# Attention with a following mixture of adapters: loads, stores and mixture steps moved to fixed places, x transposed by DMA

## The chip, the cores and the metric

One core of a Trainium2 chip. The metric is the device time of one execution in microseconds (us); lower is better. The span in a profile is about 2 us shorter than the time of the same run (286.4 against 288.2 us before), because it counts from the first to the last instruction.

Engines are named as in the profile: PE is TensorE (PEld its weight loads), DVE is VectorE, ACT is ScalarE, POOL is GpSimd. SPq is the queue of SyncE, from which nearly all DMAs are issued (36.2 of the 38.2 MB that the kernel before moves), one after another in program order.

A run over 1.5% above the fastest of its kernel is called slow here and is left out of the ratios.

## The reference, cut to what matters

```python
# B, H, S, D = 8, 8, 576, 64
scores = q @ k.T / sqrt(D) + bias_table[bucket(i - j)]   # per batch and head
x = softmax(scores) @ v                                  # [B*S, H*D] = [4608, 512]
logits = x @ w_gate                                      # 8 adapters, the 2 best are kept
out = x + sum over the 2 kept e of  w_e * (x @ A[e]) @ B[e]
```

## The kernel before

A pair is two heads of one batch; there are 32 pairs, four to a batch. Pair i goes through five groups g = 0..4 (scores of 128 keys, exp on ACT, multiplication by exp(bias) on DVE, called a band). While pair i makes its scores, TensorE also multiplies the probabilities of pair i-1 with v (`pv`), and at the end of the slot DVE normalises them into x (`norm`). A batch of x is complete after four pairs; then its twelve mixture steps are put into a list and taken from it one by one, in groups 1, 2 and 3 of the next pairs.

```python
    def load_v(b, h0, h1):                 # 16 DMAs of 64 KB
        vr = v[b, h0:h1, :S4, :].rearrange("h (t p j) d -> j t p h d", t=4, j=4)
        for j in range(4):
            for t in range(4):
                nc.sync.dma_start(out=vfs[b][j * 32:(j + 1) * 32, t, h0:h1, :],
                                  in_=vr[j, t])
    # ... cut ...
    def norm(i):
        # ... cut ...
        nc.vector.reciprocal(rc, at(acc, D, (SLOT, 5), (D1, 2)))
        rm = sp.tile([128, 5, 2], FP32, name="rm", tag="rm")
        nc.vector.tensor_tensor(rm, rc, mask, op=ALU.mult)
        nc.vector.tensor_tensor(xs[b][:, :, 2 * hp:2 * hp + 2, :], ...)   # x
    # ... cut ...
    def m_x(b, half):                      # x transposed: 8 products on PE, one DVE copy
        ps = acp.tile([128, 4, 256], BF16, name="xps", tag="acc")
        for t2 in range(2):
            for c in range(4):
                nc.tensor.transpose(ps[:, c, t2 * 128:(t2 + 1) * 128],
                                    x[:, 2 * half + t2, 2 * c:2 * c + 2, :], ident)
        nc.vector.tensor_copy(xT[:, :, half * 256:(half + 1) * 256], ps)
    # ... cut ...
    def m_out(b, t):                       # one row tile: result, then four stores of 64 KB
        o = op.tile([128, Dm], FP32, name="o", tag="o")          # 3 buffers
        nc.vector.tensor_tensor(o, ps, xs[b][:, t]..., op=ALU.add)
        for j in range(4):
            nc.sync.dma_start(out=orr[j], in_=o[j * 32:(j + 1) * 32])
    # ... cut ...
    for i in range(NPAIR + 1):
        b, hp = divmod(i, HP)
        if i < NPAIR:
            if i == 1:
                load_weights()                         # adapters A, B and the gate
            if hp == 0 and b + 1 < B:
                load_kq(b + 1, 0, H)
                load_v(b + 1, 0, H)                    # sixteen in one go
                load_tails(b + 1)
            if i + 2 < NPAIR:
                cast_kq(i + 2)                         # GpSimd
            cast_v(i)                                  # GpSimd
            if i == 2:
                cast_weights()                         # GpSimd
            if hp == 1 and b + 1 < B:
                load_vtails(b + 1)                     # GpSimd; waits for pv of two pairs ago
            if i < HP - 1:
                bias_pair(i + 1, nc.gpsimd)
        for g in range(5):
            # ... qk, transposes, pv ...
            if g in (1, 2, 3) and i > 0:
                if queue:
                    queue.pop(0)()                     # the next mixture step
```

The softmax here doesn't subtract the row's maximum and nothing guards it: scores larger than these inputs give would overflow.

## Time and profile before

289.8 us (median of the first three runs, 288.9 to 290.3).

| before | value |
|---|---|
| span of the profiled run | 286.4 us |
| busy share PE / DVE / ACT / POOL | 68 / 71 / 57 / 39% |
| start of the x tile of pair 0 / 3 / 31 | 29.8 / 56.8 / 266.0 us |
| 28 pairs, from x of pair 3 to x of pair 31 | 209.2 us |
| from the start of the last x to the end | 20.4 us |

The start times of the DVE operation that writes x, once per pair, cut the run into stages. The busy lines of the page of the kernel before:

```profile
PE 195.4 (68%) x2603; PEld 132.1 (46%) x2608; DVE 204.6 (71%) x496; ACT 163.6 (57%) x184; POOL 113.1 (39%) x218
```

No engine is full over the whole run. But in stretches without holes DVE is, and PE nearly. Next is the table of stretches; each line gives the stretch, then busy us (and instructions) of PE, PEld, DVE, ACT and POOL, the granted clock of PE, a DMA share and GB/s:

```profile
110.00:115.00 5.00, 2.08 (x31) 1.44 (x29) 0.07 (x1) 2.86 (x3) 3.02 (x5) 1.00 1.37 238
115.00:120.00 5.00, 0.00 (x0) 0.00 (x0) 0.00 (x0) 0.00 (x0) 0.00 (x0) 0.62 0.80 153
120.00:125.00 5.00, 2.18 (x19) 1.36 (x18) 4.04 (x10) 0.00 (x0) 0.00 (x0) 0.50 0.52 137
...
150.00:155.00 5.00, 4.91 (x81) 3.58 (x78) 4.97 (x11) 4.20 (x5) 3.19 (x5) 1.00 1.22 185
```

At 150 us PE and DVE are both nearly always busy. At 115 us every engine stands still for 5 us, and in the next 5 us the clock is half. Why it stands still is in the timeline of DVE, and then of SPq, around that time (start, duration, engine, line, operation; in brackets the idle time before it and what ended it):

```profile
109.38 0.68 DVE L489 TENSOR_TENSOR o<-dl,x 128x512 f32<-128x512 f32 x1
120.89 0.69 DVE L506 COPY o<-dlt 128x512 f32<-128x512 f32 x1 [10.82 <-DMA out_dram<-o]
```

```profile
105.30 12.28 SPq L92 DMA_DIRECT2D vf<-in_v_dram  x16
117.68 5.57 SPq L494 DMA_DIRECT2D out_dram<-o  x12
```

DVE has nowhere to write: its three output buffers wait for stores, and the stores wait behind sixteen v loads, which take 12.3 us to issue. The waits of all engines list this three times: two long ones, of 10.8 and 10.4 us, and one of 1.4 us at the very end. They also list a similar wait of GpSimd for the adapter weights near 40 us (engine, line, releaser: us in total, times, longest):

```profile
DVE o L506 <- DMA out_dram<-o: 22.6, 3, 10.8
...
POOL Ab L265 <- DMA A_f<-in_moe_A_dram: 8.0, 1, 8.0
```

### The profile page before, as it was taken

What the parts mean: (1) busy time and instruction counts of PE and PEld (TensorE: products, weight loads), DVE (VectorE), ACT (ScalarE), POOL (GpSimd) and SP (SyncE); (2) the same over time, 40 slices, a digit from 0 to 9 for tenths busy, and PEclk for the clock granted to TensorE, in tenths of its full rate; (3) what the DMA queues carried; (4) which work ended last, traced back from release to release, by engine and by line L of the source; (5) the groups of instructions that cost most, each with busy time, mean ns of one, the idle gap of its engine ahead of it and who ended that gap; (6) DMA issues with size and microseconds to landing.
All of it is one profiled execution on the core that took longest, in us unless ns stands there. A gap on an engine that the chain in (4) does not pass through costs nothing.

```text
span 286.4 us, 6863 instructions
## 1 busy us (share of the span) xinstructions
PE 195.4 (68%) x2603; PEld 132.1 (46%) x2608; DVE 204.6 (71%) x496; ACT 163.6 (57%) x184; POOL 113.1 (39%) x218
## 2 busy tenths in 40 slices
PE   2149760997797686089698869239689778887550
PEld 1025430665565464066466556127466555655410
DVE  5217823998998973178889887067979999889750
ACT  2238860778696746048398727307859677785000
POOL 8263906947523914005704760400923380020100
PEclk9999996699999979669799968859979999999955
DMA  8969969931397649730389549950249432401424
GB/s 156 208 153 266 221 104 286 175 58 13 64 312 115 136 113 288 151 85 2 37 283 144 134 75 299 147 144 17 18 124 278 115 86 64 117 8 39 111 73 111
DMA packets 78169, 38.17 MB, mean 133 GB/s; under 512 B 55984, under 2 KB 73400, under 8 KB 78136
## 3 DMA queue, kind: packets, MB, share of 16 engines
q1 hardware_dynamic: 65080, 36.16, 51.0%
q0 software_dynamic: 13056, 1.58, 9.5%
q8 instruction: 20, 0.33, 0.5%
q14 instruction: 13, 0.11, 0.1%
HBM read 29.84 MB, written 9.45 MB: 137 GB/s over the span
## 4 chain that ended last, share of the span: by engine, by line
DVE 35%; PE 19%; DMA 15%; SPq 15%; issue 7%; ACT 3%; POOL 3%; DVEq 0%; ACTq 0%; POOLq 0%
DMA vf<-in_v_dram 9%; PE pv L358 8%; DVE x L383 7%; SPq L92 7%; DVE kqT L281 3%; DMA out_dram<-o 3%; SPq L494 3%; DVE o L489 3%; DMA g_d<-ge 2%; DVE rm L382 2%; PE sc L315 2%; PE xps L399 2%; SPq L84 2%; PE sc L319 2%; DVE rc L380 2%
## 5 line engine op out<-in xcount | busy, mean ns | idle before, releaser
L315 PE MATMUL sc<-kqT 64*128 64x512 bf16 x256 | 53.0, 412 | 1.1 <-ACT p_286 L327 0.7
L279 PE MATMUL kqps<-ident,kqn 128*128 128x128 bf16 x256 | 23.2, 237 | 24.3 <-POOL kqn L128 19.4
L279 PEld LDWEIGHTS <-kqn 128*128 128x128 bf16 x256 | 16.1, 105 | 33.5 <-POOL kqn L128 22.4
L399 PE MATMUL xps<-ident,x 128*128 128x128 bf16 x128 | 12.7, 242 | 23.9 <-DVE o L506 18.7
L281 DVE COPY kqT<-kqps 128x1024 bf16<-128x1024 bf16 x32 | 21.8, 683 | 10.0 <-PE kqps L279 10.0
L383 DVE TENSOR_TENSOR x<-pv,rm 128x640 bf16<-128x640 f32 x32 | 26.4, 825 | 1.1
L128 POOL CAST kqn<-kf 128x512 bf16<-128x512 f32 x31 | 24.1, 776 | 5.8 <-DMA kf<-in_k_dram 5.7
L128 POOL CAST kqn<-qf 128x512 bf16<-128x512 f32 x31 | 22.1, 711 | 9.2 <-DMA qf<-in_q_dram 9.2
L489 DVE TENSOR_TENSOR o<-dl,x 128x512 f32<-128x512 f32 x32 | 21.7, 685 | 3.6 <-PE dl L487 2.3
L399 PEld LDWEIGHTS <-x 128*128 128x128 bf16 x128 | 8.5, 106 | 29.0 <-issue 22.2
L487 PE MATMUL dl<-Bb,zT 128*128 128x512 bf16 x31 | 13.1, 431 | 10.4 <-DVE zT L481 6.6
L506 DVE COPY o<-dlt 128x512 f32<-128x512 f32 x4 | 2.8, 691 | 23.4 <-DMA out_dram<-o 22.6
L315 PEld LDWEIGHTS <-kqT 64*128 64x128 bf16 x256 | 12.5, 94 | 15.0 <-issue 3.2
L319 PE MATMUL sc<-kqT,tlT 128*128 128x512 bf16 x32 | 13.1, 411 | 5.2 <-ACT p_4328 L327 0.8
L300 ACT ACTIVATE ptl<-tsc 128x512 bf16<-128x512 f32 x8 | 4.8, 594 | 19.9 <-PE tsc L297 19.9
L323 PEld LDWEIGHTS <-kqT 128*128 128x128 bf16 x128 | 10.6, 104 | 10.6 <-issue 7.2
L116 POOL DMA_DIRECT2D vt_99<-in_v_dram x8 | 4.9, 621 | 22.7 <-PE pv L358 22.7
L439 ACT ACTIVATE ex<-df 128x32 f32<-128x32 f32 (+1 forms) x12 | 2.7, 222 | 19.1 <-POOL df L433 19.1
L323 PE MATMUL sc<-tlT,kqT 128*128 128x128 bf16 x128 | 13.4, 232 | 0.0
L380 DVE RECIPROCAL rc<-pv 128x10 f32<-128x10 f32 x32 | 6.9, 216 | 8.6 <-PE pv L358 8.6
L116 POOL DMA_DIRECT2D vt_96<-in_v_dram x8 | 4.9, 618 | 19.9 <-PE pv L358 19.9
L401 DVE COPY xT<-xps 128x1024 bf16<-128x1024 bf16 x16 | 10.9, 683 | 2.1 <-PE xps L399 2.1
(792 smaller groups left out, 706.5 us busy)
## 6 DMA issues: line engine op xcount, KB each, us to landing
vf<-in_v_dram SPq DMA_DIRECT2D x128, 64.0 KB, 3.3
out_dram<-o SPq DMA_DIRECT2D x128, 64.0 KB, 1.7
kf<-in_k_dram SPq DMA_DIRECT2D x7, 1024.0 KB, 6.0
qf<-in_q_dram SPq DMA_DIRECT2D x7, 1024.0 KB, 9.3
out_dram<-o SPq DMA_DIRECT2D x8, 128.0 KB, 2.4
kf<-in_k_dram SPq DMA_DIRECT2D x1, 768.0 KB, 5.1
qf<-in_q_dram SPq DMA_DIRECT2D x1, 768.0 KB, 6.8
Mr<-g_d SPq DMA_DIRECT2D x4, 144.0 KB, 4.3
```

Source lines behind the costliest of these rows:

```text
L92: nc.sync.dma_start(out=vfs[b][j * 32:(j + 1) * 32, t, h0:h1, :], in_=vr[j, t])
L128: nc.gpsimd.tensor_copy(o, s)
L279: nc.tensor.transpose(o[:, :, j, :], n[:, w, j], ident)
L281: nc.vector.tensor_copy(t, ps)
L315: nc.tensor.matmul(sc[:, h * 512:(h + 1) * 512], lhsT=t[s, 0, g * 128:(g + 1) * 128], rhs=t[s, 1, :], start=True, stop=True)
L319: nc.tensor.matmul(sc[:, 0:512], lhsT=tt[:, 0, hp, :], rhs=t[:, 1, :], start=True, stop=True)
L323: nc.tensor.matmul(sc[:, o:o + 128], lhsT=t[:, 0, j * 128:(j + 1) * 128], rhs=tt[:, 1, hp, :], start=True, stop=True, skip_group_check=True)
L358: nc.tensor.matmul(acc[:, sl * SLOT + o:sl * SLOT + o + n], lhsT=lhsT, rhs=rhs, start=start, stop=stop, skip_group_check=True)
L383: nc.vector.tensor_tensor(xs[b][:, :, 2 * hp:2 * hp + 2, :], at(acc, 0, (SLOT, 5), (D1, 2), (1, D)), rm.unsqueeze(3).to_broadcast((128, 5, ...
L399: nc.tensor.transpose(ps[:, c, t2 * 128:(t2 + 1) * 128], x[:, 2 * half + t2, 2 * c:2 * c + 2, :], ident)
L487: nc.tensor.matmul(ps, lhsT=zT[:, t, :], rhs=Bb, start=True, stop=True)
L489: nc.vector.tensor_tensor(o, ps, xs[b][:, t].rearrange("p h d -> p (h d)"), op=ALU.add)
```

## The change

Its intent: spread the DMAs so that nothing urgent stands behind a long row of others; give every mixture step a fixed slot with a distance between dependent steps; take the transposes of x off PE and DVE by a transposing DMA; and make the first v values arrive already cast. The core of the diff, with cuts marked:

```diff
-    def load_v(b, h0, h1):
+    def load_v(b, js):                       # a quarter (four DMAs) per pair
...
-        for t2 in range(2):                  # m_x: still there, for the last batch only
+    def m_xdma(b):
+        xT = xp.tile([128, 16, 128], BF16, name="xT", tag="xT")
+        st[(b, "xT")] = xT
+        nc.sync.dma_start_transpose(
+            out=xT, in_=xs[b][:, 0:4].rearrange("p t h d -> p (t h d)"))
...
-        o = op.tile([128, Dm], FP32, name="o", tag="o")
+        if t == 0:
+            st[(b, "o")] = op.tile([128, 4, Dm], FP32, name="o", tag="o")
...
+        if t % 2 == 1:                       # stores of two row tiles at once
...
         nc.vector.reciprocal(rc, at(acc, D, (SLOT, 5), (D1, 2)))
+        between()                            # a band multiply
         rm = sp.tile([128, 5, 2], FP32, name="rm", tag="rm")
...
+    # first v values: sixteen casting loads issued by GpSimd
+            nc.gpsimd.dma_start(out=vns[0][j * 32:(j + 1) * 32, t, :, :D], in_=...)
...
+        i0 = HP * (b + 1) + 1                # slots of the mixture of batch b
+        if b < B - 1:
+            at_slot(0, 0, lambda: m_xdma(b))
+        else:
+            at_slot(0, 1, lambda: m_x(b, 0))
+            at_slot(0, 2, lambda: m_x(b, 1))
+        at_slot(1, 1, lambda: m_logits(km, st[(b, "xT")], 4))
+        # gate steps at (1,3), (1,4), (2,0), (2,1), (2,2); z at (2,1), (2,2);
+        # zT at (2,4); outputs at (3,1) to (3,4)
...
             if hp == 0 and b + 1 < B:
                 load_kq(b + 1, 0, H)
-                load_v(b + 1, 0, H)
+            if b + 1 < B:
+                load_v(b + 1, (hp,))
```

The casts of k, q and v were also spread over the groups of a pair, and the loads of k and q of batch 0 were cut into four.

More of the change, by code (lines that the diff above doesn't have):

```diff
@@ L79, in alloc_loads @@
         kfs[b] = (kf, qf)
-        vfs[b] = ldp.tile([128, 4, H, D], FP32, name="vf", tag="vf")
+        if b > 0:
+            vfs[b] = ldp.tile([128, 4, H, D], FP32, name="vf", tag="vf")
     def load_kq(b, h0, h1):
@@ L86, in load_kq @@
                 in_=src[b, h0:h1, :S4, :].rearrange("h (p j) d -> p h (j d)", j=4))
-    def load_v(b, h0, h1):
-        vr = v[b, h0:h1, :S4, :].rearrange("h (t p j) d -> j t p h d", t=4, j=4)
-        for j in range(4):
+    def load_v(b, js):
+        vr = v[b, :, :S4, :].rearrange("h (t p j) d -> j t p h d", t=4, j=4)
+        for j in js:
             for t in range(4):
-                nc.sync.dma_start(out=vfs[b][j * 32:(j + 1) * 32, t, h0:h1, :],
+                nc.sync.dma_start(out=vfs[b][j * 32:(j + 1) * 32, t, :, :],
                                   in_=vr[j, t])
@@ L119, with cast_kq @@
     kqn = {}
-    def cast_kq(i, engs=None):
+    def cast_kq(i, w, eng=None):
         b, hp = divmod(i, HP)
-        t = knp.tile([128, 2, 4, 2, D], BF16, name="kqn", tag="kqn")
-        for w in range(2):
-            o = t[:, w].rearrange("p j h d -> p h j d")
-            s = kfs[b][w][:, 2 * hp:2 * hp + 2, :].rearrange("p h (j d) -> p h j d", j=4)
-            if engs is None:
-                nc.gpsimd.tensor_copy(o, s)
-            elif engs[w] == "v":
-                nc.vector.tensor_copy(o, s)
-            else:
-                for h in range(2):
-                    nc.scalar.copy(o[:, h], s[:, h])
-        kqn[i] = t
+        if w == 0:
+            kqn[i] = knp.tile([128, 2, 4, 2, D], BF16, name="kqn", tag="kqn")
+        o = kqn[i][:, w].rearrange("p j h d -> p h j d")
+        s = kfs[b][w][:, 2 * hp:2 * hp + 2, :].rearrange("p h (j d) -> p h j d", j=4)
+        if eng is nc.scalar:
+            for h in range(2):
+                nc.scalar.copy(o[:, h], s[:, h])
+        else:
+            (eng or nc.gpsimd).tensor_copy(o, s)
     def cast_v(i):
@@ L146 @@
         nc.vector.memset(t, 0.0)
+    load_kq(0, 2, 4)
+    load_kq(0, 4, 6)
     load_tails(0)
-    load_v(0, 0, H)
-    load_kq(0, 2, H)
+    nc.vector.memset(vns[0][:, :, :, D:D1], 1.0)
+    for j in range(4):
+        for t in range(4):
+            nc.gpsimd.dma_start(
+                out=vns[0][j * 32:(j + 1) * 32, t, :, :D],
+                in_=v[0, :, t * 128:(t + 1) * 128, :]
+                .rearrange("h (p j) d -> j p h d", j=4)[j])
     C = 255
@@ L155 @@
     nc.vector.memset(g_sb, 0.0)
-    cast_kq(0, "va")
+    cast_kq(0, 0, nc.vector)
+    cast_kq(0, 1, nc.scalar)
     bsub = cp.tile([H, NB], FP32, tag="bsub")
@@ L188 @@
     MHr = cp.tile([128, HP, 192], BF16, tag="MHr")
-    for h0, h1 in ((0, 2), (2, H)):
+    for h0, h1 in ((0, 2), (2, 4), (4, H)):
         for j in range(4):
@@ L200 @@
                                 ap=[[1, 64], [1024, HP], [1, 192]]))
+        if h0 == 2:
+            load_kq(0, 6, H)
     M = cp.tile([128, H, 3, 128], BF16, tag="M")
@@ L230 @@
         nc.gpsimd.memset(vt[64:128, :, 2 * D + 1:2 * D1], 1.0)
-    for vn in vns:
-        nc.gpsimd.memset(vn[:, :, :, D:D1], 1.0)
+    nc.gpsimd.memset(vns[1][:, :, :, D:D1], 1.0)
     load_vtails(0)
@@ L372, in pv, with norm @@
         mm(0, 2 * D1, lhsT, vt[:, hp, :], False, True)
-    def norm(i):
+    def norm(i, between):
         b, hp = divmod(i, HP)
@@ L393, in m_x @@
         if half == 0:
-            st[(b, "xT")] = xp.tile([128, 4, S4], BF16, name="xT", tag="xT")
-        xT = st[(b, "xT")]
-        ps = acp.tile([128, 4, 256], BF16, name="xps", tag="acc")
-        for t2 in range(2):
-            for c in range(4):
-                nc.tensor.transpose(ps[:, c, t2 * 128:(t2 + 1) * 128],
-                                    x[:, 2 * half + t2, 2 * c:2 * c + 2, :], ident)
-        nc.vector.tensor_copy(xT[:, :, half * 256:(half + 1) * 256], ps)
+            st[(b, "xT")] = xp.tile([128, 16, 128], BF16, name="xT", tag="xT")
+        ps = acp.tile([128, 8, 128], BF16, name="xps", tag="acc")
+        for n in range(8):
+            c = n % 4
+            nc.tensor.transpose(ps[:, n, :], x[:, 2 * half + n // 4, 2 * c:2 * c + 2, :],
+                                ident)
+        nc.vector.tensor_copy(st[(b, "xT")][:, half * 8:half * 8 + 8, :], ps)
     def m_xtail(b):
@@ L416, in m_xtail, with m_logits @@
         st[(b, "xT", "t")] = xT
-    def m_gate(key, xT, nt):
+    def m_logits(key, xT, nt):
         lp = acp.tile([128, nt, E], FP32, name="lp", tag="acc")
@@ L422, in m_gate @@
             for c in range(4):
-                nc.tensor.matmul(lp[:, t, :], lhsT=xT[:, c, t * 128:(t + 1) * 128],
+                nc.tensor.matmul(lp[:, t, :], lhsT=xT[:, 4 * t + c, :],
                                  rhs=Wb[:, c, :], start=first, stop=(c == 3),
@@ L431, in m_gate @@
             nc.vector.max(out=m8[:, t, :], in_=lg[:, t, :])
-        df = sp.tile([128, nt, E], FP32, name="df", tag=f"df{nt}")
-        nc.gpsimd.tensor_tensor(df, lg, m8[:, :, 0:1].to_broadcast((128, nt, E)),
-                                op=ALU.subtract)
-        mk = sp.tile([128, nt, E], FP32, name="mk", tag=f"mk{nt}")
-        nc.vector.tensor_tensor(mk, lg, m8[:, :, 1:2].to_broadcast((128, nt, E)),
-                                op=ALU.is_ge)
-        ex = sp.tile([128, nt, E], FP32, name="ex", tag=f"ex{nt}")
@@ L439, in m_gate @@
-        nc.scalar.activation(ex, df, ACT.Exp)
-        nc.gpsimd.tensor_tensor(mk, mk, ex, op=ALU.mult)
-        st[key + ("mk",)] = mk
-    def m_gate2(key, nt):
-        mk = st.pop(key + ("mk",))
-        sm = sp.tile([128, nt], FP32, name="sm", tag=f"sm{nt}")
-        nc.vector.tensor_reduce(sm, mk, axis=AX.X, op=ALU.add)
-        nc.vector.reciprocal(sm, sm)
-        gate = sp.tile([128, nt, E], BF16, name="gate", tag=f"gate{nt}")
-        nc.gpsimd.tensor_tensor(gate, mk, sm.unsqueeze(2).to_broadcast((128, nt, E)),
-                                op=ALU.mult)
-        st[key + ("gate",)] = gate
+        st[key] = dict(lg=lg, m8=m8)
@@ new lines, in m_gate @@
+    def m_gate(key, nt, part):
+        d = st[key]
+        if part == 0:
+            df = sp.tile([128, nt, E], FP32, name="df", tag=f"df{nt}")
+            nc.gpsimd.tensor_tensor(
+                df, d["lg"], d["m8"][:, :, 0:1].to_broadcast((128, nt, E)),
+                op=ALU.subtract)
+            mk = sp.tile([128, nt, E], FP32, name="mk", tag=f"mk{nt}")
+            nc.vector.tensor_tensor(
+                mk, d["lg"], d["m8"][:, :, 1:2].to_broadcast((128, nt, E)),
+                op=ALU.is_ge)
+            d.update(df=df, mk=mk)
+        elif part == 1:
+            ex = sp.tile([128, nt, E], FP32, name="ex", tag=f"ex{nt}")
+            nc.scalar.activation(ex, d["df"], ACT.Exp)
+            d["ex"] = ex
+        elif part == 2:
+            nc.gpsimd.tensor_tensor(d["mk"], d["mk"], d["ex"], op=ALU.mult)
+        elif part == 3:
+            sm = sp.tile([128, nt], FP32, name="sm", tag=f"sm{nt}")
+            nc.vector.tensor_reduce(sm, d["mk"], axis=AX.X, op=ALU.add)
+            nc.vector.reciprocal(sm, sm)
+            d["sm"] = sm
+        else:
+            gate = sp.tile([128, nt, E], BF16, name="gate", tag=f"gate{nt}")
+            nc.gpsimd.tensor_tensor(
+                gate, d["mk"], d["sm"].unsqueeze(2).to_broadcast((128, nt, E)),
+                op=ALU.mult)
+            st[key + ("gate",)] = gate
@@ L460, in m_z @@
             for c in range(4):
-                nc.tensor.matmul(zp[:, t, :], lhsT=xT[:, c, t * 128:(t + 1) * 128],
+                nc.tensor.matmul(zp[:, t, :], lhsT=xT[:, 4 * t + c, :],
                                  rhs=Ab[:, c, :], start=(t == 0 and c == 0),
@@ L487, in m_out @@
         nc.tensor.matmul(ps, lhsT=zT[:, t, :], rhs=Bb, start=True, stop=True)
-        o = op.tile([128, Dm], FP32, name="o", tag="o")
-        nc.vector.tensor_tensor(o, ps, xs[b][:, t].rearrange("p h d -> p (h d)"),
+        if t == 0:
+            st[(b, "o")] = op.tile([128, 4, Dm], FP32, name="o", tag="o")
+        o = st[(b, "o")]
+        nc.vector.tensor_tensor(o[:, t], ps, xs[b][:, t].rearrange("p h d -> p (h d)"),
                                 op=ALU.add)
-        n0 = b * S + t * 128
-        orr = out[n0:n0 + 128, :].rearrange("(u j) d -> j u d", j=4)
-        for j in range(4):
-            nc.sync.dma_start(out=orr[j], in_=o[j * 32:(j + 1) * 32])
+        if t % 2 == 1:
+            n0 = b * S + (t - 1) * 128
+            orr = out[n0:n0 + 256, :].rearrange("(t u j) d -> j u t d", t=2, j=4)
+            for j in range(4):
+                nc.sync.dma_start(out=orr[j], in_=o[j * 32:(j + 1) * 32, t - 1:t + 1])
     def m_outt(b):
@@ L504, in m_outt @@
                              start=False, stop=(e == 1), skip_group_check=True)
-        o = op.tile([128, Dm], FP32, name="o", tag="o")
+        o = op.tile([128, Dm], FP32, name="ot", tag="ot")
         nc.vector.tensor_copy(o, ps)
@@ L509, in m_outt, with mixture, at_slot, both @@
             nc.sync.dma_start(out=out[n0:n0 + 64, :], in_=o[e * 64:(e + 1) * 64])
-    def pieces(b):
+    events = {}
+    def mixture(b):
         km, kt = (b, "m"), (b, "t")
         tail = b % 2 == 1
-        def xT(t=None):
-            return st[(b, "xT", "t") if t else (b, "xT")]
-        def step(f, ft=None):
-            def run():
-                f()
-                if tail and ft:
-                    ft()
-            return run
-        return [
-            step(lambda: m_x(b, 0)),
-            step(lambda: m_x(b, 1)),
-            step(lambda: None, lambda: m_xtail(b)),
-            step(lambda: m_gate(km, xT(), 4), lambda: m_gate(kt, xT(1), 1)),
-            step(lambda: m_gate2(km, 4), lambda: m_gate2(kt, 1)),
-            step(lambda: m_z(km, xT(), 0)),
-            step(lambda: m_z(km, xT(), 1)),
-            step(lambda: m_zT(km, 4), lambda: m_z(kt, xT(1), 2)),
-            step(lambda: m_out(b, 0), lambda: m_zT(kt, 1)),
-            step(lambda: m_out(b, 1)),
-            step(lambda: m_out(b, 2)),
-            step(lambda: m_out(b, 3), lambda: m_outt(b)),
-        ]
+        i0 = HP * (b + 1) + 1
+        def at_slot(di, g, f, only_tail=False):
+            if tail or not only_tail:
+                events.setdefault(5 * (i0 + di) + g, []).append(f)
+        def both(f):
+            f(km, 4)
+            if tail:
+                f(kt, 1)
+        if b < B - 1:
+            at_slot(0, 0, lambda: m_xdma(b))
+        else:
+            at_slot(0, 1, lambda: m_x(b, 0))
+            at_slot(0, 2, lambda: m_x(b, 1))
+        at_slot(0, 4, lambda: m_xtail(b), True)
+        at_slot(1, 1, lambda: m_logits(km, st[(b, "xT")], 4))
+        at_slot(1, 1, lambda: m_logits(kt, st[(b, "xT", "t")], 1), True)
+        for n, g in enumerate((8, 9, 10, 11, 12)):
+            at_slot(0, g, lambda n=n: both(lambda k, nt: m_gate(k, nt, n)))
+        at_slot(2, 1, lambda: m_z(km, st[(b, "xT")], 0))
+        at_slot(2, 2, lambda: m_z(km, st[(b, "xT")], 1))
+        at_slot(2, 3, lambda: m_z(kt, st[(b, "xT", "t")], 2), True)
+        at_slot(2, 4, lambda: m_zT(km, 4))
+        at_slot(3, 0, lambda: m_zT(kt, 1), True)
+        at_slot(3, 1, lambda: m_out(b, 0))
+        at_slot(3, 2, lambda: m_out(b, 1))
+        at_slot(3, 3, lambda: m_out(b, 2))
+        at_slot(3, 4, lambda: m_out(b, 3))
+        at_slot(4, 4, lambda: m_outt(b), True)
@@ L541 @@
     NPAIR = B * HP
-    queue = []
+    for b in range(B):
+        mixture(b)
     late = None
@@ L545 @@
     tail_transposes(0)
-    cast_kq(1)
+    cast_kq(1, 0)
+    cast_kq(1, 1)
     for i in range(NPAIR + 1):
@@ L554 @@
                 load_kq(b + 1, 0, H)
-                load_v(b + 1, 0, H)
                 load_tails(b + 1)
-            if i + 2 < NPAIR:
-                cast_kq(i + 2)
-            cast_v(i)
+            if b + 1 < B:
+                load_v(b + 1, (hp,))
             if i == 2:
@@ L568 @@
                 qk(i, g)
-            if g == 0 and i + 1 < NPAIR:
-                transposes(i + 1)
+                if g == 0 and b > 0:
+                    cast_v(i)
+                if g in (1, 2) and i + 2 < NPAIR:
+                    cast_kq(i + 2, g - 1)
             if g == 0 and i < NPAIR and hp == 0:
                 tail_scores(b)
-            if g in (1, 2, 3) and i > 0:
-                if queue:
-                    queue.pop(0)()
-                pv(i - 1, g - 1)
+            if g == (0 if i > 3 else 3) and i + 1 < NPAIR:
+                transposes(i + 1)
+            for f in events.pop(5 * i + g, ()):
+                f()
+            for sl in ((), (0,), (1,), (2, 3), (4,))[g] if i > 0 else ():
+                pv(i - 1, sl)
             if g == 3 and hp == HP - 1 and b + 1 < B:
@@ L579 @@
             if g == 4 and i > 0:
-                pv(i - 1, 3)
-                pv(i - 1, 4)
-                norm(i - 1)
-                if i % HP == 0:
-                    queue += pieces(i // HP - 1)
-            if late:
+                norm(i - 1, late or (lambda: None))
+            elif late:
                 late()
@@ L594, in late @@
                         tail_band(i // HP)
-    for f in queue:
-        f()
+    for key in sorted(events):
+        for f in events[key]:
+            f()
 _INS = ['q', 'k', 'v', 'bias_table', 'moe_w_gate', 'moe_A', 'moe_B']
```

## The prediction

> **What bounds it now.** The span is 286.4 us; no engine is full (VectorE 71%, TensorE 68%, ScalarE 57%, GpSimd 39%). Where nothing blocks, a head pair with mixture work takes 5.7 to 5.9 us (finished x tiles in the timeline, 150.04 to 155.80) with VectorE busy 4.9 of every 5 us (stretch table): VectorE bounds the good stretches. The rest is holes:
> - 39 to 49 us: GpSimd waits 8.0 us for the adapter weights, queued behind sixteen v loads (14.5 us of issue); bias tiles and casts stand behind it.
> - 110 to 121 and 181 to 190 us: VectorE waits for an output buffer (waits: o on out_dram, 22.6 us in 3), because stores stand behind sixteen v loads.
> - After each hole the granted clock is 0.50 for some 5 us.
> - Once per batch mixture steps wait for one another on TensorE (1.3 us twice), and a band multiply takes 2.1 instead of 0.41 us, five times, under three GpSimd casts back to back. [...]
>
> **What the change does.**
> 1. v loads come four per pair, weights after the first four; `o` holds a batch. The three holes go: 28 us, plus 2 us of slow clock each: about 32 us.
> 2. Mixture steps in fixed slots, a dependent step at least one group later: 1 to 2 us a batch, about 10 us in all.
> 3. x transposed by DMA for seven batches of eight: VectorE loses 14 copies of 0.68 us (9.6 us), TensorE 112 transposes about 0.06 us apart (7 us). About 5 us on the path.
> 4. A band multiply between the reciprocal and its use: about 2 us.
> 5. Start: sixteen casting loads on GpSimd at about 0.63 us (as its other loads take) are 10 us, so pair 1's cast comes at about 21 instead of 18 us; the bias table comes earlier (its store issues at about 8 instead of 11 us). These cancel: x of pair 0 at about 29 us, as before.
> 6. End: same chain, about 20 us after the last x.
>
> **Cost.** The DMA transpose of 512 KB must be back about 6 us after x. [...] Four v loads (3.3 us to land) and stores stand just ahead. [...]
>
> **Sum.** 289.8 - 32 - 10 - 5 - 2 + 7 = about 248 us. From the other side: x of pair 3 at 46 us, 28 pairs at 6.3, 20 us of end, 3 of launch: 245. Prediction 248 us, 80% range 233 to 268. Chances: faster by over 2% 0.94, within 2% 0.03, slower 0.03.
>
> **What would show it.** No wait of VectorE for stores; no wait over 3 us for the weights; clock 1.0 from 30 us to the end of the pairs; x tiles 5.6 to 6.4 us apart; VectorE busy about 193 us; x of pair 0 at 28 to 31 us, of pair 31 at 220 to 228; [...], any stall standing on the gate logits' first product.
>
> **What would make it wrong.** [...] The sixteen casting loads take much longer, delaying pair 1. VectorE and GpSimd collide more as both get denser. The start keeps a hole for the weights.

The sum came to 248 us. Its term + 7 is the estimate of TensorE's stall behind the DMA transposes.

## The result, and the profile after

256.3 us median (255.4 to 257.9, 4 runs); before in the same rounds 289.4. The ratio is 0.886 (95% interval 0.881 to 0.892). A ratio is the mean time of one kernel's fast runs over that of the other's of the same rounds, so it is not quite the ratio of the medians. To compare kernels of different rounds I multiply each ratio by 288.4 us, about the median of before; the changed kernel is then 255.6 us.

| | before | after | predicted |
|---|---|---|---|
| time, us | 289 | 256.3 | 248 (233 to 268) |
| x of pair 0, us | 29.8 | 32.6 | 28 to 31 |
| x of pair 3, us | 56.8 | 52.7 | 46 |
| 28 pairs, us | 209.2 | 184.2 | 176 |
| end after the last x, us | 20.4 | 17.6 | 20 |
| busy DVE, us | 204.6 | 195.0 | 193 |

The busy line of the page after:

```profile
PE 187.8 (74%) x2496; PEld 123.7 (49%) x2496; DVE 195.0 (77%) x483; ACT 162.7 (64%) x184; POOL 117.3 (46%) x229
```

The wait of DVE for stores is gone from the list. Stores and four v loads now take turns (timeline of SPq):

```profile
103.63 4.10 SPq L523 DMA_DIRECT2D out_dram<-o  x6
107.77 2.33 SPq L93 DMA_DIRECT2D vf<-in_v_dram  x4
110.21 1.90 SPq L404 DMA_TRANSPOSE xT<-x  x1
```

The weights are waited for about half as long as before, and a new wait has come, of the first product that needs the transposed x (waits):

```profile
PE lp L438 <- DMA xT<-x: 11.9, 6, 3.1
...
POOL Ab L273 <- DMA A_f<-in_moe_A_dram: 4.5, 1, 4.5
```

One instance in full, batch 1. First DVE, then SPq, then PE in the timeline after:

```profile
76.90 0.82 DVE L392 TENSOR_TENSOR x<-pv,rm 128x640 bf16<-128x640 f32 x1
```

```profile
78.67 1.99 SPq L93 DMA_DIRECT2D vf<-in_v_dram  x4
80.76 2.48 SPq L404 DMA_TRANSPOSE xT<-x  x1
```

```profile
82.01 0.39 PE L323 MATMUL sc<-kqT 64*128 64x512 bf16 x2
85.46 0.56 PE L438 MATMUL lp<-Wb,xT 128*128 128x8 bf16 x16 [3.06 <-DMA xT<-x]
```

x is complete at 77.7 us. The queue first finishes its stores and issues four v loads, so the transpose is issued 3.0 us after x was ready, at 80.76. It lands 4.66 us later by the chain that ended last, at 85.42, and the logits start at 85.46. TensorE has then stood idle for 3.06 us. The stretches after it show what follows (columns as above):

```profile
82.00:86.00 4.00, 0.94 (x25) 0.64 (x24) 1.76 (x5) 1.51 (x2) 0.00 (x0) 1.00 0.91 180
86.00:90.00 4.00, 4.00 (x54) 2.90 (x51) 2.67 (x12) 2.15 (x3) 1.46 (x3) 0.65 0.41 94
90.00:94.00 4.00, 4.00 (x54) 2.50 (x53) 3.41 (x12) 3.90 (x6) 2.36 (x7) 0.93 0.98 312
```

The clock is 0.65 in the mean of the next 4 us: it falls to 0.50 at 87.2 us, 1.7 us after the logits started, and stays there for 3.4 us. PE is now full (4.00 of 4 us) at a low clock, and DVE, which should be the limit, idles a third of the time (busy 2.67 of 4 us). Here a gap of 3.06 us was followed by the low clock; this instance alone does not show that the gap brought it.

The clock records show more than this one instance. After 50 us and until the pairs end, the clock of this kernel falls seven times, each time to 0.50 for 3.4 us (the last time for 6.8), and the falls stand a multiple of 3.41 us apart. In the 3.41 us before each fall PE was busy 44 to 62%. Three of the seven have a wait for the transposed x in those 3.41 us (3.06, 1.30 and 3.09 us), four have none; x_on_pe, below, has no such wait and still falls twice. So it need not be a stop of 3 us: before the four falls without that wait PE was busy 44 to 57% of the 3.41 us. What decides whether the clock falls is not shown.

### The profile page after: what moved, and what is told of

The parts are those of the page before. It is cut to its first block, busy times and chain, and to the rows that moved or that the text cites. A ratio compares the mean times of both kernels' runs of the same rounds, so it can differ in the third digit from the quotient of the medians.

```text
span 254.5 us, 6519 instructions
## 1 busy us (share of the span) xinstructions
PE 187.8 (74%) x2496; PEld 123.7 (49%) x2496; DVE 195.0 (77%) x483; ACT 162.7 (64%) x184; POOL 117.3 (46%) x229
## 4 chain that ended last, share of the span: by engine, by line
PE 43%; DVE 32%; DMA 13%; POOL 7%; issue 2%; ACT 1%; DVEq 0%; POOLq 0%; ACTq 0%
PE pv L366 17%; DMA xT<-x 11%; PE sc L323 9%; DVE p L350 6%; DVE x L392 6%; DVE o L517 5%; PE zp L487 3%; DVE p L342 3%; DMA tl<-in_q_dram 3%; DVE rm L391 3%; PE dl L513 3%; PE kqps L287 3%; DVE kqT L289 2%; POOL vn L152 2%; DVE tlT L298 2%
## 5 line engine op out<-in xcount | busy, mean ns | idle before, releaser
L335 ACT ACTIVATE p<-sc 128x1024 bf16<-128x1024 f32 x160 | 155.8, 1024 | 65.7 <-PE sc L323 36.1
L366 PE MATMUL pv<-vn,p 128*128 128x65 bf16 (+1 forms) x1152 | 68.2, 206 | 12.6 <-DVE x L392 12.5
L366 PEld LDWEIGHTS <-p 128*128 128x128 bf16 x1280 | 59.0, 104 | 37.4 <-issue 18.9
L350 DVE TENSOR_TENSOR p<-p,M 128x512 bf16<-128x512 bf16 (+1 forms) x128 | 66.2, 533 | 3.3 <-POOL M L223 2.7
L366 PE MATMUL pv<-vt,p 128*128 128x130 bf16 x128 | 29.8, 232 | 2.4 <-DVE p L342 2.4
L453 POOL TENSOR_TENSOR df<-lg,m 128x32 f32<-128x32 f32 (+1 forms) x12 | 3.5, 293 | 60.6 <-DVE lg L443 31.8
L287 PEld LDWEIGHTS <-kqn 128*128 128x128 bf16 x256 | 15.8, 101 | 24.6 <-POOL kqn L132 11.3
L117 POOL DMA_DIRECT2D vt<-in_v_dram x16 | 9.8, 621 | 32.6 <-PE pv L366 32.6
L137 POOL CAST vn<-vf 128x512 bf16<-128x512 f32 x28 | 20.5, 733 | 0.0
L342 DVE TENSOR_TENSOR p<-p,M 128x256 bf16<-128x256 bf16 x32 | 18.5, 579 | 0.1
L327 PE MATMUL sc<-kqT,tlT 128*128 128x512 bf16 x32 | 13.7, 427 | 0.0
L438 PE MATMUL lp<-Wb,xT 128*128 128x8 bf16 x128 | 4.5, 167 | 11.9 <-DMA xT<-x 11.9
## 6 DMA issues: line engine op xcount, KB each, us to landing
qf<-in_q_dram SPq DMA_DIRECT2D x7, 1024.0 KB, 10.2
```

Source lines behind the costliest of these rows:

```text
L137: nc.gpsimd.tensor_copy(vns[b % 2][:, :, h, :D], vfs[b][:, :, h, :])
L287: nc.tensor.transpose(o[:, :, j, :], n[:, w, j], ident)
L335: nc.scalar.activation(p, sc, ACT.Exp, scale=scale)
L342: nc.vector.tensor_tensor(p[:, 384:640], p[:, 384:640], M4[:, hp, :], op=ALU.mult)
L350: nc.vector.tensor_tensor(o, o, Mh[:, :, x0 * 128:(x0 + b1 - b0) * 128], op=ALU.mult)
L366: nc.tensor.matmul(acc[:, sl * SLOT + o:sl * SLOT + o + n], lhsT=lhsT, rhs=rhs, start=start, stop=stop, skip_group_check=True)
```

## The experiments

Twelve kernels ran, all with correct results. "28 pairs" and the x times are read from each run's own profile. The profiles marked * fell in a slow run, so their stage times are some per cent too long. The intervals reach 1.5 to 3.5 us to either side, so the kernels between 243 and 246 us are not told apart. Leaving out slow runs favours a kernel that scatters more: by the medians of all runs the six fastest lie 8 to 11.5 us under the changed kernel, not 10 to 12.

| kernel | runs, us (median) | ratio to before (95%) | x 288.4 | x of pair 3 | 28 pairs |
|---|---|---|---|---|---|
| after | 256.3 | 0.886 (0.881-0.892) | 255.6 | 52.7 | 184.2 |
| b_loads | 270.0 | 0.926 (0.920-0.932) | 267.0 | 49.2 | 195.0 |
| b_stores | 259.2 | 0.899 (0.893-0.905) | 259.2 | 56.3 | 182.2 |
| b_both | 255.5 | 0.877 (0.869-0.885) | 252.9 | 49.9* | 187.2* |
| x_on_pe | 246.2 | 0.845 (0.835-0.855) | 243.7 | 51.8 | 173.3 |
| x_dummy | 248.2 | 0.847 (0.839-0.855) | 244.2 | 52.9* | 178.6* |
| x_first | 245.6 | 0.851 (0.844-0.857) | 245.3 | 53.3* | 176.3* |
| logits_late | 254.6 | 0.886 (0.880-0.892) | 255.5 | 51.1 | 181.6 |
| vt_late | 260.9 | 0.903 (0.895-0.911) | 260.4 | 54.1 | 187.6 |
| pe_vt | 246.2 | 0.849 (0.842-0.856) | 244.9 | 53.6 | 172.8 |
| w_late | 252.9 | 0.871 (0.864-0.878) | 251.2 | 52.5 | 179.5 |
| best_pe | 247.2 | 0.852 (0.844-0.860) | 245.7 | 52.3 | 176.2 |
| best_dma | 244.8 | 0.844 (0.832-0.855) | 243.3 | 52.3 | 172.2 |

### Parts of the change put into the kernel before

**b_loads**: the v loads four at a time.

```diff
                 load_kq(b + 1, 0, H)
-                load_v(b + 1, 0, H)
                 load_tails(b + 1)
+            if b + 1 < B:
+                load_v(b + 1, (hp,))
```

> The kernel before with one part of the change: v loads issued four at a time per pair (the weights then stand behind four of them, not sixteen). Theory H (the three holes are queueing on the one issue queue): the weight hole at 39 to 49 us shrinks to under 4 us and the store waits of VectorE (22.6 us) fall to under 5 us, since at most four loads stand ahead of a store: 258 to 266 us. Rival: the output buffers are the limit, not the queue; then only the weight hole goes: 276 to 281 us.

Measured: 267.0 us by the ratio, one us outside the range of theory H and far from its rival. The weight hole shrank as said (x of pair 3 at 49.2 instead of 56.8 us). The wait for stores did not fall under 5 us but to 14.9, because the stores still find four v loads and the large k and q loads ahead of them, and then take 7.8 us to issue, twelve of them (SPq, 94.7 to 107.7 us). Waits of b_loads:

```profile
DVE o L506 <- DMA out_dram<-o: 14.9, 3, 6.8
```

**b_stores**: an output tile per batch, stores of two row tiles.

```diff
-        o = op.tile([128, Dm], FP32, name="o", tag="o")
+        if t == 0:
+            st[(b, "o")] = op.tile([128, 4, Dm], FP32, name="o", tag="o")
...
+        if t % 2 == 1:
...
-        o = op.tile([128, Dm], FP32, name="o", tag="o")      # m_outt: the rows left over
+        o = op.tile([128, Dm], FP32, name="ot", tag="ot")
```

> The kernel before with one part of the change: an output tile for a whole batch, and stores of two row tiles at once. Theory H: the weight hole stays, the two long waits for an output buffer go, with their slow clock: 265 to 271 us. Rival: the steps behind then wait for something else in the same queue (the stores still stand behind sixteen v loads, so the next user of the batch tile waits): 280 us or more.

Measured: 259.2 us, better than expected by theory H. This part alone is worth 29 us. The two batches with the long store holes went from 40.3 and 40.4 us to 30.3 and 28.8 (x to x over four pairs); two other batches, 27.6 and 27.7, went to 24.8 each. These two follow directly on the long holes: in the kernel before, the slow clock reaches 4 us into each of them and returns once more for 3.4 us (at 140 and 208 us); b_stores shows neither. I had counted only the long waits and 2 us of slow clock each.

No wait of DVE for stores is left, although sixteen v loads still stand in one row in the queue. So the buffers were as much the limit as the queue. The edit has three parts that were not taken apart: the deeper buffer, half as many stores, and a tile of its own for the rows left over, on which both long waits stood (L506).

**b_both**: the two edits together.

```diff
+            if b + 1 < B:
+                load_v(b + 1, (hp,))
...
+            st[(b, "o")] = op.tile([128, 4, Dm], FP32, name="o", tag="o")
```

> The kernel before with both: loads spread and stores in batch tiles. Theory H with the prediction's 32 us: 255 to 260 us, as fast as the whole change, whose other parts then sum to nothing (slots gain what the DMA transpose loses). Rival (the slots and the shorter VectorE work carry much of the gain): 263 us or more.

Measured: 252.9 us by the ratio, below the expected range. The two DMA parts alone are at least as fast as the whole change. They overlap: 21 and 29 us alone, 35.5 us together. The rest of the change therefore adds nothing in sum, and the next runs show that this zero is a gain and a loss.

### The DMA transpose

**x_on_pe**: the changed kernel with x of all batches transposed on PE.

```diff
-        if b < B - 1:
+        if False:
             at_slot(0, 0, lambda: m_xdma(b))
```

> The changed kernel, but x of all eight batches is transposed by TensorE and copied by VectorE, as before. Theory A (the DMA transpose's latency stalls TensorE at the first gate-logits product about 2 us in each of seven batches, 12 to 14 us in all, about as much as it saves): 252 to 258 us, no stall on the logits, VectorE busy about 9 us more. Rival B (the DMA transpose is a real part of the gain, because VectorE bounds the stretches): 262 us or more. Rival C (it is a net loss): under 251.

Measured: 243.7 us, 12 us faster than the changed kernel. (The medians of all runs give 10 us; two of its four runs count as slow.) Rival C holds: the DMA transpose is a net loss, and theory A, which is about the wait, had put its cost too low. The same stretches as above, in x_on_pe:

```profile
82.00:86.00 4.00, 3.24 (x59) 2.39 (x56) 3.79 (x10) 3.64 (x4) 0.00 (x0) 1.00 0.65 146
86.00:90.00 4.00, 4.00 (x66) 2.77 (x65) 3.59 (x17) 3.13 (x6) 1.47 (x4) 1.00 0.65 168
90.00:94.00 4.00, 4.00 (x71) 3.18 (x70) 3.80 (x11) 3.66 (x5) 3.40 (x8) 1.00 1.07 356
```

DVE is busy 3.6 to 3.8 of every 4 us and the clock stays at 1.00, though both engines have more to do. The sum of (1 - clock) over 2 us stretches, from 50 us to 20 us before the end, is 13.7 us in the changed kernel and 3.4 us here.

**x_dummy**: as x_on_pe, but the seven DMA transposes are issued as well, into a tile that nobody reads.

```diff
         if b < B - 1:
             at_slot(0, 0, lambda: m_xdma(b))      # now into a tile xU
-        else:
-            at_slot(0, 1, lambda: m_x(b, 0))
-            at_slot(0, 2, lambda: m_x(b, 1))
+        at_slot(0, 1, lambda: m_x(b, 0))
+        at_slot(0, 2, lambda: m_x(b, 1))
```

> The changed kernel with x transposed by TensorE for all batches, as in x_on_pe, and the seven DMA transposes issued as well, into a tile that nobody reads. Theory A (what costs about 12 us is that TensorE waits for the transposed tile and then runs at half clock; the transfer itself is harmless): 241 to 247 us, like x_on_pe. Rival (the transposes cost by holding the issue queue or the DMA engines, so other loads and stores come late): 250 us or more.

Measured: 244.2 us, the same as x_on_pe within the interval. So it is not the transfer, nor the queue it occupies, that costs 12 us. What is left is that the mixture steps need its result. TensorE had the logits started 5.2 to 5.9 us after x was complete here; in the changed kernel the transposed x landed only 7.3 to 8.4 us after x in five of the six batches whose landing is recorded. That the wait is the whole cost is not shown: see logits_late.

**x_first**: the four v loads of that pair are issued after the transpose.

```diff
-            if b + 1 < B:
+            if b + 1 < B and hp != 1:
                 load_v(b + 1, (hp,))
...
             for f in events.pop(5 * i + g, ()):
                 f()
+            if g == 0 and hp == 1 and b + 1 < B:
+                load_v(b + 1, (hp,))
```

> The changed kernel, but in the pair of the transpose the four v loads are issued after it instead of ahead of it. Theory A: what makes the transpose late is its place in the issue queue (SyncE issues four v loads, 2 us, after x is ready), so it is issued about 2 us earlier, the stall on the logits falls from 14 to under 4 us, and the time is 246 to 250 us. Rival B: the stall is hidden behind VectorE, so the time stays at 254 to 257 us although the stall goes.

Measured: 245.3 us by the ratio, 10 us faster than the changed kernel, under the low end of what theory A said. But the stall did not fall under 4 us: it is 7.7 us in 5 waits in the profiled run, a slow one, because the transpose itself now landed 5.7 us after its issue (median) instead of 4.4 us. Waits of x_first:

```profile
PE lp L438 <- DMA xT<-x: 7.7, 5, 2.6
```

So most of the gain came with a stall that is one third smaller, not gone. The sum of lost clock is half, 6.8 us. Whether the waits cost more than their own length, by the slow clock that follows some of them, is not shown by a run of its own: only three of the seven falls in the changed kernel come with such a wait. Lost clock alone does not order the kernels either: it is 10.2 us in the profile of x_dummy (a slow run without any such wait) and 5.1 us in logits_late, next.

**logits_late**: all steps from the logits on two groups later (logits at (1,3), z at (2,3) and (2,4), outputs at (3,3) to (4,1)).

```diff
-        at_slot(1, 1, lambda: m_logits(km, st[(b, "xT")], 4))
+        at_slot(1, 3, lambda: m_logits(km, st[(b, "xT")], 4))
```

> The changed kernel, but logits and every later mixture step of a batch stand two groups (about 2.4 us) later. Theory A: the stall on the logits goes and 6 to 12 us with it: 244 to 250 us. Rival B: VectorE bounds the pairs anyway: 254 to 257 us. A delay of the end does not follow, since the last batch's steps come after the last pair as before.

Measured: 255.5 us by the ratio, unchanged. The stall is gone from the waits altogether, yet Theory A's gain did not come; the time is the one that Rival B named. This run shows a second kind of wait. Here is the worst instance, DVE and then POOL in the timeline of logits_late:

```profile
180.22 4.37 DVE L391 TENSOR_TENSOR rm<-rc,mask 128x10 f32<-128x10 f32 x1
184.63 0.83 DVE L392 TENSOR_TENSOR x<-pv,rm 128x640 bf16<-128x640 f32 x1
```

```profile
179.39 1.23 POOL L117 DMA_DIRECT2D vt<-in_v_dram  x2 [2.79 <-PE pv L366]
180.60 0.65 POOL L137 CAST vn<-vf 128x512 bf16<-128x512 f32 x1
181.15 0.64 POOL L132 CAST kqn<-kf 128x512 bf16<-128x512 f32 x1
181.71 0.64 POOL L132 CAST kqn<-qf 128x512 bf16<-128x512 f32 x1
182.27 0.64 POOL L137 CAST vn<-vf 128x512 bf16<-128x512 f32 x1
182.83 0.62 POOL L132 CAST kqn<-kf 128x512 bf16<-128x512 f32 x1
183.39 0.62 POOL L132 CAST kqn<-qf 128x512 bf16<-128x512 f32 x1
183.95 0.62 POOL L137 CAST vn<-vf 128x512 bf16<-128x512 f32 x1
```

A multiply of ten columns, normally 0.16 us, took 4.37 us and ended (at 184.59 us) as the seventh cast in an unbroken row ended (at 184.57). TensorE had no work ready behind it and stood idle for 5.5 us (timeline of PE):

```profile
186.10 0.59 PE L513 MATMUL dl<-Bb,zT 128*128 128x512 bf16 x1 [5.46 <-DVE kqT L289]
```

The multiply did not end between two casts, of 0.62 to 0.65 us each, but with the last. By the recorded starts it began 0.4 us before the first of them (180.22 against 180.60), while GpSimd was issuing the two v tail loads. What held it is not recorded, so that the casts did is an inference from these times. GpSimd has such a row of casts because it first waits, at the load of the v tails, for TensorE (2.79 us here; 32.6 us in six waits in the changed kernel) and then works off what has gathered.

### The rows of casts

To size this I summed, for DVE's multiplies after 50 us whose two inputs lie in SBUF, the time over their usual one (an estimate from the traces; usual is 0.28, 0.42 and 0.55 us for bands of 256, 512 and 768 columns): 16.7 us before, 19.7 after, 13.8 in x_on_pe, 23.7 in logits_late. These are the multiplies whose times spread: in the changed kernel the one of ten columns took 0.15 to 1.95 us and the bands of 256 columns 0.28 to 2.51, but the one that writes x, which reads PSUM, 0.82 to 0.83 in all 32 instances. (A recount that also takes in the small multiply, usually 0.16 us, gives 18.4, 19.8, 15.3 and 24.6: the figures are good to about 1.5 us, and their order holds.)

**vt_late**: the changed kernel with the v tails loaded one pair later, so that GpSimd waits less.

```diff
-            if hp == 1 and b + 1 < B:
+            if hp == 2 and b + 1 < B:
                 load_vtails(b + 1)
```

> The changed kernel, but GpSimd issues the loads of the v tails one pair later, so it does not stop there for TensorE and then run a backlog of casts in one go. Theory G (VectorE multiplies with two inputs in SBUF wait for a whole unbroken row of GpSimd casts, 19.7 us over their usual time after 50 us, and half of that reaches the end): that excess falls to 8 to 12 us and the time to 246 to 251 us. Rival (the excess is hidden, or the casts form another row elsewhere): 254 to 257 us.

Measured: the excess fell to 11.7 us (12.9 in the recount), about as theory G said, and the time rose to 260.4 us. The gain that theory G promised did not come. But the run is no clean test of it: the excess fell at the bands (15.5 to 5.7 us in the recount) and rose at the small multiply ahead of x (4.3 to 7.3), and the wait for the transposed x grew (waits of vt_late):

```profile
PE lp L438 <- DMA xT<-x: 15.2, 7, 3.9
```

**pe_vt**: the same edit on x_on_pe, where no such wait exists.

```diff
-        if b < B - 1:
+        if False:
             at_slot(0, 0, lambda: m_xdma(b))
...
-            if hp == 1 and b + 1 < B:
+            if hp == 2 and b + 1 < B:
                 load_vtails(b + 1)
```

> x_on_pe with the v tails loaded one pair later, as in vt_late. vt_late took 8 us off the excess of VectorE's multiplies and was 4 us slower, with longer waits for the DMA transpose. If the excess only matters once the transpose's wait is gone (VectorE bounds): 236 to 241 us. Rival (the excess is hidden here too, or the order on GpSimd delays something else): 242 to 248 us.

Measured: 244.9 us; x_on_pe is 243.7. The excess fell from 13.8 to 10.5 us with no effect on the time that these runs can resolve. The rival's time came. But here too the row that matters was not removed. Beside six casts in a row the small multiply took 3.6 us, against 2.0 at most in x_on_pe, and TensorE then stood idle for 3.1 us (DVE in the timeline of pe_vt; vt_late has the same, 3.6 and 3.0 us):

```profile
171.18 3.63 DVE L391 TENSOR_TENSOR rm<-rc,mask 128x10 f32<-128x10 f32 x1
```

So the two runs show that taking excess off the bands bought nothing. They do not show that a long row is harmless when it hits the multiply on which everything waits. In the profile of logits_late the batch with the 4.4 us multiply took 29.2 us and the next one, which begins in the slow clock, 27.2; in x_on_pe they took 25.4 and 24.6. These two make 6.4 of the 8.3 us by which its 28 pairs are longer. That is read from one profile of each and not tested; no run took the row of casts apart.

### The start

**w_late**: the adapter weights cast two pairs later.

```diff
-            if i == 2:
+            if i == 4:
                 cast_weights()
```

> The changed kernel, but the adapter weights are cast two pairs later. The hole that is left between x of pair 1 (37.5 us) and x of pair 2 (48.2 us) should go if it comes from GpSimd waiting 4.5 us for the weights: x of pair 2 at 43 to 44 us, time 250 to 252 us. Rival: the loads of the first batches are then late anyway (the queue is full till then), and the hole only moves to pair 3 or 4: 255 to 257 us.

Measured: 251.2 us by the ratio, within the range that I gave to the theory. The reason is not the one that I gave. x of pair 3 is at 52.5 us, against 52.7. GpSimd now stops a few operations later, at the first v values of batch 1 (timeline of POOL in w_late):

```profile
44.16 0.77 POOL L137 CAST vn<-vf 128x512 bf16<-128x512 f32 x1 [2.54 <-DMA vf<-in_v_dram]
```

The hole moved, as the rival said. All the time that this run gained lies after pair 3, where its edit does nothing, so I take the 4 us as not explained by the edit. Two of its four runs, which count as slow, were 254.5 and 255.4 us, close to the changed kernel.

**best_pe**: x_on_pe, the late cast of the weights, and pair 1's casts on DVE and ACT, so that GpSimd need not issue its sixteen casting loads first.

```diff
     gt = g_d.ap()
+    cast_kq(1, 0, nc.vector)
+    cast_kq(1, 1, nc.scalar)
...
-    cast_kq(1, 0)
-    cast_kq(1, 1)
```

> x_on_pe, the weights cast two pairs later as in w_late, and pair 1's first casts on VectorE and ScalarE in place of GpSimd, which issues sixteen casting loads until 16 us. If the three gains add (12, about 4, and 3 to 5 us of earlier start): 234 to 239 us, x of pair 0 at 27 to 29 us, x of pair 3 under 47 us. Rival (the start then waits for the bias tiles or the next loads): x of pair 3 at 49 us or later, 240 to 244 us.

Measured: 245.7 us, x of pair 0 at 34.1 us and of pair 3 at 52.3. The rival is right, though the time is above its range too: the gains do not add, and the start did not get shorter. Pair 3 stands at 51 to 54 us in the changed kernel and in all nine experiments made from it, whichever wait of the start is removed. In best_pe GpSimd waits 4.27 us for v values at 45 us. What sets this time as a whole stays open; all these loads share one queue.

**best_dma**: x_first with the same two edits of the start.

```diff
+            if g == 0 and hp == 1 and b + 1 < B:
+                load_v(b + 1, (hp,))         # after the transpose
...
+    cast_kq(1, 0, nc.vector)
+    cast_kq(1, 1, nc.scalar)
...
+            if i == 4:
                 cast_weights()
```

> x_first with the same two further edits as best_pe. It tells whether the DMA transpose, issued ahead of the v loads, can do as well as TensorE: by theory A some stall and slow clock remain, so 1 to 4 us slower than best_pe: 237 to 243 us. Rival (the freed VectorE and TensorE time pays): equal or faster than best_pe.

Measured: 243.3 us, not told apart from x_on_pe or best_pe, so the 1 to 4 us of theory A did not come. The wait for the transposed x is 5.9 us in 5 waits here. So a DMA transpose issued directly after x, ahead of other loads, is as good as TensorE within what these runs resolve. It is not shown to be better. Whether the work taken off DVE and TensorE pays for the waits that are left was not taken apart.

x_on_pe, x_dummy, x_first, pe_vt, best_pe and best_dma beat both the kernel before (by 15%) and the changed kernel (by 4 to 5%).

## Why the prediction was right or wrong

The time of 256.3 us lies in the range, 8 us above the centre of 248, and the direction was given 0.94. That it came no further out is in part luck: the DMA transpose cost 10 us more than the sum said, and the holes gave 3.5 us more. The sum, term by term; measured terms are differences of the column "x 288.4" along the path before, b_both, x_on_pe, after:

| term of the prediction | predicted | measured |
|---|---|---|
| holes of loads and stores | -32 | -35.5 (before to b_both) |
| slots, the band in norm, the new start | -10 - 2 + 0 = -12 | -9.2 (b_both to x_on_pe) |
| DMA transpose: gain and stall | -5 + 7 = +2 | +11.9 (x_on_pe to after) |

1. **The holes: right in cause, a little small.** DVE's wait for stores is gone, and b_both shows that the two DMA parts carry 35.5 us. Stores matter more than I thought (29 us alone): beside the long waits, slow clock in the batches that follow went with them. "No wait over 3 us for the weights" was wrong: 4.5 us, and w_late shows that behind it stands the next load of the same queue.
2. **Slots: about right in size, together with the band in norm and the start.** These three were not taken apart. The trace says that the start lost 2 to 3 us (x of pair 0 at 32.6 us, in b_loads, with the old start, at 30.5), so slots and norm gained more than 9.2. The two us of the band in norm were not tested.
3. **The DMA transpose: the term that was mis-sized.** The prediction put 7 us of stall into the sum; that was an estimate, and part of what it was worked out from stood in no trace of this case. The trace of the changed kernel shows 4.4 us from issue to landing for the 512 KB ([128 x 2048] bf16; 4.4 to 4.7 us where it is recorded, 4.3 to 5.7 in x_dummy), and the issuing queue was held 1.7 to 2.9 us by one (1.7 to 3.0 in x_dummy). With the queue's delay ahead of it, 3.0 us in batch 1, x landed 7.3 to 8.4 us after it was complete in five batches. The stall that follows from it was sized too small: 11.9 us in six waits, up to 3.1 us each, instead of 7. I also did not charge slow clock for it, as I had for the holes (13.7 us of lost clock against 3.4 in x_on_pe, though only three of the seven falls come with such a wait). And I credited 5 us for work taken off DVE and TensorE; no run shows this gain by itself. The stall alone is as large as the net loss, so relief and slow clock may cancel; how the 12 us divide is not shown.
4. **The start.** "These cancel" was wrong by 3 us at pair 0, and x of pair 3 came at 52.7 us instead of 46. Pair 1's cast came at 22 us (predicted 21), which explains one us of it; the wait for the weights does not explain the rest, since w_late and best_pe take it away and pair 3 stays at 52. The cause stays open. The end was 2.4 us shorter than assumed. It came with the part on stores: b_stores and b_both have the shorter end too (18.1 and 18.3 us), b_loads does not (20.4).
5. **"Clock 1.0 from 30 us to the end of the pairs"** was wrong: one fall at 43 us and seven after 50 us, in part for the reason of point 3. "VectorE busy about 193 us" was right (195.0). X of pair 31 came at 236.9 us (predicted 220 to 228), and the transpose landed 4.4 us after its issue.

## What to carry to other kernels

When everything goes through one issue queue, ask of each transfer what stands ahead of it at the moment when its data is ready: splitting a row of sixteen loads and giving stores more buffer was worth 35 us, and the place of one transpose behind four loads cost some 10 us. Moving work to the DMA saved nothing here while its result was awaited on the critical path; check the time from "input ready" to "landed" (7.3 to 8.4 us in five batches here), not the transfer's own (4.4 us), and leave the slack accordingly. When you bundle several edits, take the bundle apart on the chip afterwards: here a part of 12 us in the wrong direction was hidden in a gain of 33.
